# The last output piece of an attention kernel: 128 columns copied by VectorE in place of 256 copied by ScalarE

## Chip, core, metric

The kernel runs on one NeuronCore of a Trainium2 chip. The metric is device microseconds (us) of that core, median of several executions. Time before the change: 343.14 us (three runs, 342.83 to 343.26).

## The reference

Two independent attention blocks A and B with the same shapes; the outputs are concatenated along the last axis.

```python
# B, Sq, D = 16, 32, 1024;  Hq, Hkv, Sk, Dh = 32, 4, 512, 128;  all bf16
q = (x @ wq).reshape(B, Sq, Hq, Dh).transpose(0, 2, 1, 3)
k = repeat(k_cache, 8, axis=1); v = repeat(v_cache, 8, axis=1)
p = softmax(einsum("bhqd,bhkd->bhqk", q, k) * Dh ** -0.5)
o = einsum("bhqk,bhkd->bhqd", p, v)
out = o.transpose(0, 2, 1, 3).reshape(B, Sq, Hq * Dh) @ wo        # (16, 32, 1024)
# result: concatenate([out_A, out_B], -1)
```

## The kernel before

A generator `stream()` feeds projection matmuls into TensorE between the attention matmuls. Its last units are the output projection of B, token tile by token tile. A unit multiplies all 32 heads' `oT` blocks (each loaded as weights) with up to 512 columns of `wo`, sums in PSUM, copies the sum to SBUF as bf16 and writes it out.

```python
outp = enter(tc.tile_pool(name="outp", bufs=2))
...
def f_units(pr, tt, n0, width, eng):
    ps = psum.tile([P, NW], FP32, name="f_ps", tag="proj")        # P = 128, NW = 512
    nh, off = divmod(n0, NW)
    for h in range(HQ):                                           # HQ = 32
        ...
        nc.tensor.matmul(ps[:, 0:width], lhsT=oT[pr, tt][:, h, :],
                         rhs=wo_tiles[pr, nh, h // REP][:, h % REP, off:off + width],
                         start=(h == 0), stop=(h == HQ - 1))
        if h == HQ - 1:
            o_sb = outp.tile([P, NW], BF16, name="o_sb")
            nc.scalar.copy(out=o_sb[:, 0:width], in_=ps[:, 0:width])
            ...
            eng.dma_start(out=out_flat[tt * P:(tt + 1) * P, c0:c0 + width], in_=o_sb[:, 0:width])
        yield
...
    yield from f_units(1, TT - 1, 0, NW, nc.sync)                 # the last three units
    yield from f_units(1, TT - 1, NW, QW, nc.sync)                # QW = 256
    yield from f_units(1, TT - 1, NW + QW, QW, nc.scalar)
```

After that every engine compares one number (`ok`, a check of the softmax sums) and branches: in the normal case over a long general path to the end of the program. So each engine that has run out of work takes one branch.

```python
tc.mark_branch_hint_location("general", "LikelyTaken",
    [nc.scalar.engine, nc.vector.engine, nc.tensor.engine, nc.gpsimd.engine])
ok = nc.values_load(ok_i[0:1, 0:1], ...)
run(units, 1 << 20)                       # the rest of stream(), the pieces above among it
...
with tc.If(ok < total, preferred_fallthrough_block=True, label="general"):     # line 678
    general_path(tc, problems, out_flat)
```

## Time and profile before

The page of the profiled execution: the span, busy time per engine, the chain that ended last by engine, and two groups (line, engine, operation, tiles, shapes, count, then busy us and mean ns of one, then idle time before them).

```profile
span 341.2 us, 5454 instructions
...
PE 335.2 (98%) x2082; PEld 213.6 (63%) x2121; DVE 265.5 (78%) x336; ACT 185.9 (54%) x209; POOL 46.7 (14%) x206
...
PE 98%; issue 1%; ACT 0%; ACTq 0%
...
L320 PE MATMUL f_ps<-wo_sb,oT 128*128 128x512 bf16 (+1 forms) x525 | 128.2, 366 | 0.6
...
L329 ACT CAST o_sb<-f_ps 128x512 bf16<-128x512 f32 (+1 forms) x17 | 9.5, 559 | 23.6 <-PE f_ps L320 23.6
```

The kernel is bound by TensorE (PE). The change can only win in what follows its last matmul. The timeline of the tail (start and duration in us, engine, line, operation):

```profile
336.34 1.80 PE L320 MATMUL f_ps<-wo_sb,oT 128*128 128x256 bf16 x15
...
338.22 0.37 ACT L329 CAST o_sb<-f_ps 128x256 bf16<-128x256 f32 x1 [3.12 <-PE f_ps L320]
338.62 0.37 ACTq L331 DMA_DIRECT2D out_dram<-o_sb  x1
```

The last output matmul ends at 338.14; this moment is called T below. Copy, issue of the write, then nothing in the timeline until the span ends at 341.22: T + 3.08. What fills the rest is seen in the DMA view, here for the window T - 1.2 to T + 2.8 us (40 slices of 0.1 us: busy tenths of the 16 DMA engines; then queues with packets and MB; then the write with its size and the us from issue to landing).

```profile
DMA  0050000000000000000000000188200300000000
...
q10 hardware_dynamic: 144, 0.07, 5.5%
q8 instruction: 1, 0.02, 1.5%
q14 instruction: 1, 0.01, 0.8%
...
out_dram<-o_sb ACTq DMA_DIRECT2D x1, 64.0 KB, 1.6
```

The 144 packets on q10 are the last write: 128 rows of 512 bytes and 16 semaphore updates, inferred to be one per DMA engine (16 of each; the shares are of 8 rows, 128 / 16, and one update). They pass in slices 26 to 29. A landing is the moment at which such an update arrives; I count a write as complete with the last of its 16, because SyncE's closing wait ended 0.016 us behind that one here (landings at T + 1.947 to 2.102).

### The profile page before, as it was taken

To read this page: it belongs to the slowest core of one execution; us is meant where nothing else is said; L and a number is where in the kernel's file an instruction comes from. 1 tells how busy PE (TensorE), PEld (TensorE's weight loads), DVE (VectorE), ACT (ScalarE), POOL (GpSimd) and SP (SyncE) were. 2 spreads that over 40 slices of the span, in tenths; PEclk is the share of its full clock that TensorE was granted. 3 is DMA by queue.
4 is the path that set the end of the run, shared out by engine and by line. 5 is a ranking of instruction groups with operands and counts; after the bars stand their busy time and mean duration, and the time that the engine had idled before them with its cause. 6 is when DMAs were issued, how large, how long until landed. Compare 5 with 4: busy or idle time off the path is not lost.

```text
span 341.2 us, 5454 instructions
## 1 busy us (share of the span) xinstructions
PE 335.2 (98%) x2082; PEld 213.6 (63%) x2121; DVE 265.5 (78%) x336; ACT 185.9 (54%) x209; POOL 46.7 (14%) x206
## 2 busy tenths in 40 slices
PE   8999999999999999999999999999999999999996
PEld 6455666666666666666666666666666666666555
DVE  1046988888988898888888988879888888889540
ACT  3058666666667667666645545555555555555110
POOL 0001110011111111110012221222122101111100
PEclk9999999999999999999999999999999999999999
DMA  7999999999996987899999955998449997430001
GB/s 211 287 190 273 285 249 202 233 242 268 291 248 154 232 242 219 210 314 299 308 306 258 250 125 144 334 268 242 118 103 296 356 187 176 104 97 16 18 18 33
DMA packets 128094, 71.70 MB, mean 210 GB/s; under 512 B 75840, under 2 KB 127296, under 8 KB 128064
## 3 DMA queue, kind: packets, MB, share of 16 engines
q1 hardware_dynamic: 127264, 70.07, 84.1%
q0 software_dynamic: 384, 1.05, 0.9%
q8 instruction: 17, 0.28, 0.3%
q10 hardware_dynamic: 416, 0.20, 0.2%
q14 instruction: 13, 0.11, 0.1%
HBM read 50.86 MB, written 2.10 MB: 155 GB/s over the span
## 4 chain that ended last, share of the span: by engine, by line
PE 98%; issue 1%; ACT 0%; ACTq 0%
PE f_ps L320 32%; PE q_ps L301 28%; PE ob L425 17%; PE s_ps L357 16%; PE q_ps L534 4%; PE q_ps L516 1%; PE xT_ps L524 0%; ACT o_sb L329 0%; ACTq L329 0%
## 5 line engine op out<-in xcount | busy, mean ns | idle before, releaser
L365 ACT ACTIVATE p_sb<-s_ps,shift 128x1024 bf16<-128x1024 f32 x128 | 142.7, 1115 | 97.5 <-PE s_ps L357 88.1
L376 DVE TRANSPOSE_TENSOR_REDUCE parts<-p_sb 128x32 f32<-128x1024 bf16 x128 | 158.7, 1240 | 21.0 <-ACT p_sb L365 19.3
L320 PE MATMUL f_ps<-wo_sb,oT 128*128 128x512 bf16 (+1 forms) x525 | 128.2, 366 | 0.6
L301 PE MATMUL q_ps<-xT,wq_sb 128*128 128x512 bf16 x430 | 113.2, 379 | 0.5
L425 PE MATMUL ob<-p_sb,v_sb 128*128 128x256 bf16 x512 | 76.8, 273 | 0.8
L357 PE MATMUL s_ps<-qT,kT 128*128 128x256 bf16 x512 | 76.8, 273 | 0.0
L320 PEld LDWEIGHTS <-oT 128*128 128x128 bf16 x544 | 53.2, 98 | 35.3
L357 PEld LDWEIGHTS <-kT 128*128 128x128 bf16 x512 | 56.9, 113 | 28.3
L301 PEld LDWEIGHTS <-wq_sb 128*128 128x128 bf16 x448 | 43.8, 98 | 32.2
L425 PEld LDWEIGHTS <-v_sb 128*128 128x128 bf16 x512 | 50.1, 98 | 20.0
L447 DVE TENSOR_TENSOR oT<-r,ob 128x512 bf16<-128x512 f32 x64 | 43.9, 686 | 19.9 <-PE ob L425 19.4
L411 DVE STREAM_TRANSPOSE r<-rall 128x512 f32<-128x512 f32 x64 | 44.2, 691 | 1.1
L309 ACT CAST qT<-q_ps 128x512 bf16<-128x512 f32 x56 | 32.7, 583 | 16.5 <-PE q_ps L301 16.5
L394 POOL COPY half<-cs 64x32 f32<-64x32 f32 x32 | 6.5, 204 | 231.8 <-DVE cs L384 231.8
L329 ACT CAST o_sb<-f_ps 128x512 bf16<-128x512 f32 (+1 forms) x17 | 9.5, 559 | 23.6 <-PE f_ps L320 23.6
L534 PE MATMUL q_ps<-xT,w_sb 128*128 128x512 bf16 (+1 forms) x65 | 14.4, 379 | 0.1
L384 DVE TENSOR_REDUCE cs<-parts 128x32 f32<-128x128 f32 x32 | 12.1, 377 | 1.1
L406 DVE RECIPROCAL rall<-sums 128x32 f32<-128x32 f32 x32 | 10.2, 319 | 3.3 <-POOL sums L403 3.3
L534 PEld LDWEIGHTS <-w_sb 128*128 128x128 bf16 x67 | 6.8, 102 | 7.0 <-DMA w_sb<-in_A_wq_dram 0.2
L560 DVE CAST qT<-q_ps 128x512 bf16<-128x512 f32 x4 | 2.5, 684 | 10.2 <-PE q_ps L534 10.2
L331 POOL DMA_DIRECT2D out_dram<-o_sb x8 | 4.6, 574 | 29.3 <-ACT o_sb L329 29.3
L395 POOL TENSOR_TENSOR half<-half,cs 64x32 f32<-64x32 f32 x32 | 7.8, 243 | 2.6
(25 smaller groups left out, 44.7 us busy)
## 6 DMA issues: line engine op xcount, KB each, us to landing
v_sb<-in_A_v_cache_dram SPq DMA_DIRECT2D x16, 512.0 KB, 5.7
wq_sb<-in_B_wq_dram SPq DMA_DIRECT2D x8, 1024.0 KB, 5.7
wo_sb<-in_A_wo_dram SPq DMA_DIRECT2D x8, 1024.0 KB, 7.4
v_sb<-in_B_v_cache_dram SPq DMA_DIRECT2D x16, 512.0 KB, 4.7
wo_sb<-in_B_wo_dram SPq DMA_DIRECT2D x8, 1024.0 KB, 8.1
wq_sb<-in_A_wq_dram SPq DMA_DIRECT2D x5, 1024.0 KB, 5.8
wq_sb<-in_A_wq_dram SPq DMA_DIRECT2D x2, 512.0 KB, 6.7
kT<-in_A_k_cache_dram SPq DMA_TRANSPOSE x64, 4.4
```

The lines of the kernel that those rows point to most:

```text
L301: nc.tensor.matmul(ps[:], lhsT=w[:, dc, (h % 4) * DH:(h % 4 + 1) * DH], rhs=xT[pr][:, dc, :], start=(dc == 0), stop=(dc == DC - 1),)
L309: nc.scalar.copy(out=qT[pr, g][:, :, hl, :], in_=ps[:].rearrange("p (b s) -> p b s", s=SQ),)
L320: nc.tensor.matmul(ps[:, 0:width], lhsT=oT[pr, tt][:, h, :], rhs=wo_tiles[pr, nh, h // REP][:, h % REP, off:off + width], start=(h == 0), ...
L357: nc.tensor.matmul(s_ps[:, c, :], lhsT=kT[:, i % GRP, c, :], rhs=qT[pr, g][:, b, :, :].rearrange("p h s -> p (h s)"), start=True, stop=True,)
L365: nc.scalar.activation(out=p_sb[:], in_=s_ps[:], func=ACTF.Exp, bias=shift[:], scale=SCALE)
L376: nc.vector.tensor_reduce(out=parts[k][:, q, :, :].rearrange("p c h -> p (c h)"), in_=st[i]["p"][:].rearrange("p c (h s) -> p (c h) s", s=SQ),
L384: nc.vector.tensor_reduce(out=cs[:], in_=parts.pop(k)[:].rearrange("p q c h -> p q h c"), axis=AX.X, op=ALU.add,)
L406: nc.vector.reciprocal(out=rall[:, k, :], in_=quad.pop(k)[:])
L411: nc.vector.transpose(out=r[:].rearrange("p n s -> p (n s)"), in_=rall[:, k, o * 2 * REP:(o + 1) * 2 * REP] .unsqueeze(2).to_broadcast([P, ...
L425: nc.tensor.matmul(ob[j][:, q, :], lhsT=v_sb[:, i % GRP, c, :], rhs=st[i]["p"][:, c, :], start=(c == 0), stop=(c == KC - 1),)
L447: nc.vector.tensor_tensor(out=out, in0=rcp.pop(j)[:].rearrange("p (q h) s -> p q h s", h=REP), in1=ob.pop(j)[:].rearrange("p q (h s) -> p ...
L534: nc.tensor.matmul(first_q[h][:, ts], lhsT=w0[dc // HC][:, dc % HC, h * DH:(h + 1) * DH], rhs=xT[0][:, dc, ts], start=(dc == 0 and t0 == 0 ...
```

## The change

The last piece becomes 128 columns and is copied by VectorE; the piece ahead takes 384. Intent: half the width makes the copy shorter, and the copy is exposed.

```diff
-            def f_units(pr, tt, n0, width, eng):
+            def f_units(pr, tt, n0, width, eng, copy=nc.scalar.copy):
...
-                        nc.scalar.copy(out=o_sb[:, 0:width], in_=ps[:, 0:width])
+                        copy(out=o_sb[:, 0:width], in_=ps[:, 0:width])
...
-                yield from f_units(1, TT - 1, NW, QW, nc.sync)
-                yield from f_units(1, TT - 1, NW + QW, QW, nc.scalar)
+                yield from f_units(1, TT - 1, NW, NW - P, nc.sync)
+                yield from f_units(1, TT - 1, 2 * NW - P, P, nc.scalar, nc.vector.tensor_copy)
```

## The prediction

> **What bounds it now.** The chain of waits is 98% PE (page, part 4); PE is busy 335.2 of 341.2 us at clock 1.00. The change touches only the tail. Timeline there: the 512-wide piece's last matmul leads into two 256-wide pieces of 32 matmuls, which start every 109 ns without a gap (331.10 to 337.98 us); the last matmul's modelled end is 338.14. Then, exposed: 0.08 us until ACT starts the copy (338.22; elsewhere ACT and DVE follow PE by 0.037), 0.373 us copy (128x256), 0.03 us to the DMA issue on ACT's queue (338.62), 0.37 us issue, 0.5 us until the first packet (339.50), 0.35 us of packets (144 on that queue, about 27 ns each over 16 engines), 0.4 us until SP's wait is released (340.26), and 0.96 us of closing barriers. So about 3.1 us follow PE, and only the copy and the transfer in it can change.
>
> **What changes.**
> - PE: 32 matmuls of 384 and 32 of 128 columns for 64 of 256. Starts are 215.7 ns apart at 512 columns and 109.2 at 256, so a line gives 162.5 at 384 and 56 at 128. The warm transposes at 6.8 us, 128 columns with a fresh weight load each, do start every 56 ns, so a weight load (98 ns long, overlapped) need not slow the stream. 32 x (162.5 + 56) = 6.99 us against 6.99: no change. [...]
> - Tail copy: ACT 128x256, 373 ns, becomes DVE 128x128. DVE's fp32 PSUM copy of 512 columns took 684 ns, its bf16 ones 291 (256) and 424 (512), a fixed part near 155 ns; [...]estimate 155 + 128 x 1.04 = about 285 ns. ACT itself would need about 265 (373 and 587 extrapolated). So the width saves, not the engine: -0.09 us.
> - Waits: the DVE copy waits on eight DMA semaphores, PE and ACT. Those are old writers and readers of its buffer, done long before; DVE is idle from 330.3 us, so they are off the chain. PE to DVE should be the same 0.08 us, DVE to ACT's queue 0.03.
> - DMA: still 128 rows, 256 instead of 512 bytes. Issue and packet count stay, so hardly shorter. [...]no 256-byte output write is in this trace. I allow 0 to +0.15 us.
> - The 384-wide piece ends about 1.7 us later: matmuls to 336.4, ACT copy about 0.48, issue until about 337.3, landed near 338.6. Ahead of the last landing (340.26), so off the chain.
>
> **Sum.** 0 (PE) - 0.09 (copy) + 0.04 (transfer) = -0.05 us. Predicted 343.1 us, 8 in 10 between 342.7 and 343.6. Faster by over 2%: 0.5%; within 2%: 99%; slower: 0.5%.
>
> **Right if** the timeline shows 128-column matmuls starting every 56 ns, PE's end within 0.05 us of before, the DVE copy at 0.27 to 0.30 us, starting 0.08 us after PE's end, and first packet to SP's release staying near 0.75 us.
>
> **Wrong if** PE spaces the 128-column pairs by 70 ns or more (PE end +0.5 us or later); if DVE works through its many waits after PE's end rather than before (+0.3 us); if 256-byte writes complete noticeably later; or if DVE's late branch ends after SP's final wait. The run-to-run spread, 0.4 us, is larger than the expected gain, so the sign may not be readable.

The +0.04 for the transfer, out of the allowance of 0 to +0.15, was the author's estimate, and no trace showed it; so was the +0.3 for late waits. The 1.04 ns per column of the copy agree with the trace of before: (684 - 155) / 512 = 1.03.

## The result

The changed kernel took 344.26 us (six runs, 344.03 to 344.95) against 343.2 us (six runs, 342.83 to 343.48): 1.0034 times as long, 95% interval 1.0021 to 1.0047. Ratios here are the mean time of one kernel's fast runs over that of the other's fast runs of the same rounds, so not quite the ratio of the medians quoted. It is within 2%, but slower by 1.06 us in the medians where 0.1 us less was predicted, and outside the stated range.

The page after, which is of the slowest of the six runs (344.95 us), first the lines that answer to those of before:

```profile
span 343.0 us, 5497 instructions
...
PE 337.9 (99%) x2121; PEld 212.6 (62%) x2121; DVE 265.8 (77%) x337; ACT 185.7 (54%) x208; POOL 46.7 (14%) x206
...
DVE 0%
DVE o_sb L329 0%
...
L320 PE MATMUL f_ps<-wo_sb,oT 128*128 128x512 bf16 (+2 forms) x544 | 132.3, 366 | 0.0
...
L329 ACT CAST o_sb<-f_ps 128x512 bf16<-128x512 f32 (+1 forms) x16 | 9.2, 577 | 22.2 <-PE f_ps L320 22.2
```

The chain breaks off at VectorE's copy, because the view puts that copy's wait down to TensorE's sequencer. It is the ordinary wait for the last matmul. The larger PE busy time is a count of records: the trace of before lacks 39 matmul records (2082 of 2121). The timeline of the tail:

```profile
337.26 1.78 PE L320 MATMUL f_ps<-wo_sb,oT 128*128 128x128 bf16 x29
337.34 0.48 ACT L329 CAST o_sb<-f_ps 128x384 bf16<-128x384 f32 x1 [4.61 <-PE f_ps L320]
...
337.84 0.34 SPq L331 DMA_DIRECT2D out_dram<-o_sb  x1
339.14 0.29 DVE L329 CAST o_sb<-f_ps 128x128 bf16<-128x128 f32 x1 [9.37 <-PEq L678]
339.46 0.37 ACTq L331 DMA_DIRECT2D out_dram<-o_sb  x1
```

T is 339.04 here, and the span ends at 343.05: T + 4.01 in place of T + 3.08. The DMA view for the window T - 1.2 to T + 2.8:

```profile
DMA  0000000039968000000000000660103010000000
...
q10 hardware_dynamic: 144, 0.03, 3.9%
q8 instruction: 1, 0.02, 1.8%
q14 instruction: 2, 0.02, 1.3%
...
out_dram<-o_sb SPq DMA_DIRECT2D x1, 96.0 KB, 1.6
out_dram<-o_sb ACTq DMA_DIRECT2D x1, 32.0 KB, 2.6
```

Half the bytes take 2.6 us from issue to landing instead of 1.6. And there are two instruction packets on q14 in this window instead of one. Term by term, in us, from the records of the two traces and of a second profile of the changed kernel (the run after_again below, there the fastest of five, 343.95 us). The prediction counts its last two terms from the release of SyncE's wait, which follows the last landing by 0.02 us; hence 0.98 here for its 0.96:

```
                                   before   predicted   after   after_again
T to start of the copy              0.080     0.08      0.094      0.092
copy                                0.373     0.285     0.292      0.292
end of copy to issue                0.030     0.03      0.031      0.033
issue                               0.368     0.37      0.368      0.367
end of issue to first packet        0.506     0.5       0.508      0.505
first packet to last landing        0.745   0.75-0.9    1.735      1.424
last landing to end of span         0.978     0.98      0.978      0.979
sum: T to end of span               3.080     3.0-3.15   4.006      3.692
```

One line is wrong, by 0.7 to 1.0 us; all others hold within 0.015 us.

The spans of the two profiles differ by 1.83 us, of which 0.93 is this tail. The other 0.90 arose before the first output matmul (at 169.75 us before, 170.65 after; from there to T both took 168.39 us). In the trace's clock records the full TensorE clock was granted at 5.09 us in the one and 6.63 in the other. Over the 13 profiles (of 14) with such a record (T 337.93 to 339.04) T is earliest where the grant came earliest (3.72 us) and latest where it came latest (6.63). As this part lies ahead of all changed code, I take it for spread from run to run and not for part of the change; no run tests that. It blurs all times below by 1 us or so; the tail after T, from the profiles, is the sharper measure.

What the packets of the last write show: of its 128 rows 120 pass between T + 1.29 and T + 1.55 us, as they should. The remaining 8, with one of the 16 semaphore updates, by that count one DMA engine's share, begin only at T + 1.986. One instruction packet on q14, of 8192 bytes, lies at T + 1.682 to T + 1.989 in the same trace. In the trace of before no instruction packet falls between T and the end of the write's packets. The records also show the branch of each engine (line 678): VectorE's ended at T - 8.54 us before and at T + 0.20 after, because its copy now comes ahead of the branch; TensorE's at T - 1.71 and T - 0.75. Some 1.1 us after a branch of VectorE, and 0.72 to 0.81 us after TensorE's, an instruction packet follows: q14, 8192 bytes, and q8, 16384 bytes. (Which engine a fetch belongs to is inferred from this fixed distance, which all experiments repeated; VectorE's in this one profile came after 1.48 us.) SyncE takes the same branch, but no instruction packet follows its branch in any of the 14 profiles; it is the one engine that is missing from the branch hint's list in the source above.

### The profile page after: what moved, and what is told of

It reads as the page before. It is cut to its first block, busy times and chain, and to the rows that moved or that the text cites. A ratio compares the mean times of both kernels' runs of the same rounds, so it can differ in the third digit from the quotient of the medians.

```text
span 343.0 us, 5497 instructions
## 1 busy us (share of the span) xinstructions
PE 337.9 (99%) x2121; PEld 212.6 (62%) x2121; DVE 265.8 (77%) x337; ACT 185.7 (54%) x208; POOL 46.7 (14%) x206
## 5 line engine op out<-in xcount | busy, mean ns | idle before, releaser
L320 PE MATMUL f_ps<-wo_sb,oT 128*128 128x512 bf16 (+2 forms) x544 | 132.3, 366 | 0.0
L301 PE MATMUL q_ps<-xT,wq_sb 128*128 128x512 bf16 x448 | 116.9, 379 | 0.0
L320 PEld LDWEIGHTS <-oT 128*128 128x128 bf16 x544 | 52.0, 98 | 36.7
L534 PE MATMUL q_ps<-xT,w_sb 128*128 128x512 bf16 (+1 forms) x67 | 15.4, 390 | 0.2 <-DMA w_sb<-in_A_wq_dram 0.2
```

The costliest lines, as they stand in the source:

```text
L301: nc.tensor.matmul(ps[:], lhsT=w[:, dc, (h % 4) * DH:(h % 4 + 1) * DH], rhs=xT[pr][:, dc, :], start=(dc == 0), stop=(dc == DC - 1),)
L320: nc.tensor.matmul(ps[:, 0:width], lhsT=oT[pr, tt][:, h, :], rhs=wo_tiles[pr, nh, h // REP][:, h % REP, off:off + width], start=(h == 0), ...
L534: nc.tensor.matmul(first_q[h][:, ts], lhsT=w0[dc // HC][:, dc % HC, h * DH:(h + 1) * DH], rhs=xT[0][:, dc, ts], start=(dc == 0 and t0 == 0 ...
```

## The experiments

Three theories. F: VectorE's late branch brings an instruction fetch that holds one DMA engine just when the last write arrives. S: 256-byte writes complete later. P: TensorE's own fetch does it, which is later because its last 32 pairs pass faster (56 ns apart instead of 109). The first two experiments undo one half of the change each. The diffs below are cuts: against the changed kernel, but those of dve256, late_touch, early_touch and pe_late against the kernel before.

**act128: the width alone**

```diff
-  yield from f_units(1, TT - 1, 2 * NW - P, P, nc.scalar, nc.vector.tensor_copy)
+  yield from f_units(1, TT - 1, 2 * NW - P, P, nc.scalar)
```

> The changed kernel with ScalarE copying the last 128 columns again: the width part of the change alone. Theory F (fetch): in the changed kernel VectorE takes its final branch only after the last copy, and the instruction fetch that follows a branch by about 1.07 us holds one of the 16 DMA engines just when the last output packets reach it; with ScalarE copying, VectorE branches 8 us earlier, so F expects 343.1 us (343.2 before, minus 0.1 for the shorter copy), 16 landings close together. Rival S (size): 256-byte writes finish about 1 us later than 512-byte ones; expects 344.2. Rival P: TensorE's own fetch, 1.9 us later because the last 32 weight and matmul pairs pass faster, is in the way; expects 344.2 as well.

Measured: 343.55 us, ratio to before 0.9999 (0.9985 to 1.0013). No 8 packets stay behind. The last landing is at T + 2.395, the other 15 by T + 1.864; the span ends at T + 3.37. So S falls: the write has 256-byte rows and its time is that of before, and 15 of its 16 landings are earlier than any of before (1.947 to 2.102). F's expectation was missed in one point: it had all 16 landings close together, and one is 0.53 us behind the others. P can explain that part at most: TensorE's fetch lasted until T + 1.367 here, past the first packets (T + 1.252). No rows are held, but a few are slow, up to 0.153 us where most take 0.018, and the last update of the write passes only at T + 1.722.

**dve256: the engine alone**

```diff
-  yield from f_units(1, TT - 1, NW + QW, QW, nc.scalar)
+  yield from f_units(1, TT - 1, NW + QW, QW, nc.scalar, nc.vector.tensor_copy)   # 256 and 256, as before
```

> Two last pieces of 256 columns as before, the last one copied by VectorE: the engine part alone. F: VectorE's fetch falls about 1.2 us after the end of the matmuls, the packets of the last write about 1.4 to 1.75 us after it (copy about 0.42 us); the fetch was held up until 1.7 us in the changed kernel, so F expects a delay of the same kind, 0.2 to 1.1 us slower than before, 343.4 to 344.3. S and P expect 343.25 (only a copy longer by 0.05 us).

Measured: 344.03 us, ratio 1.0014 (1.0001 to 1.0027). VectorE's fetch is at T + 1.304 to 1.892, one engine's 8 packets begin at T + 1.889, the last landing is at T + 2.906 and the span ends at T + 3.885, 0.80 later than before; the copy itself (0.424 us) is 0.05 longer. VectorE's part alone, with 512-byte rows and TensorE's fetch out of the way (over by T - 0.03), does nearly all of the damage.

**own_tile: one wait instead of ten on VectorE's copy**

```diff
+  o_last = const.tile([P, P], BF16, name="o_last")
-  o_sb = outp.tile([P, NW], BF16, name="o_sb")
+  o_sb = own if own is not None else outp.tile([P, NW], BF16, name="o_sb")    # own=o_last for the last piece
```

> The changed kernel with the last 128 columns copied by VectorE into a buffer of its own, so that this copy waits for one semaphore (TensorE) and VectorE's sequencer can pass it and branch about 8 us earlier, as TensorE's does. F expects 343.05 us (copy 0.08 shorter, one wait fewer), the fetch near 331.5 us in the trace, the 16 landings together. S and P expect 344.2.

Measured: 343.81 us, ratio 1.0009 (0.9997 to 1.0021). The premise failed: TensorE's branch ends ahead of its last matmul (T - 0.75 in after), but VectorE did not branch ahead of its waiting copy, its branch ended at T + 0.135, so the collision stayed (fetch T + 1.241 to 1.735, the 8 packets from T + 1.731, last landing T + 2.613, end T + 3.59). As a test of the theories it tells nothing new. It did show that the copy starts at T + 0.037 when it waits for one semaphore, instead of T + 0.094.

**hold: useless work on VectorE after its copy**

```diff
+  junk = const.tile([P, 20], FP32, name="junk")
   run(units, 1 << 20)
+  for n in range(20):
+      nc.vector.memset(junk[:, n:n + 1], 0.0)
```

> The changed kernel with 20 one-column memsets on VectorE after its copy, work that nobody waits for: VectorE's branch comes 0.5 to 1.5 us later, so its fetch should come after the packets of the last write (over 1.7 us after the end of the matmuls). F expects 343.1 to 343.5 us, faster than the changed kernel although more is done. S and P expect 344.2 or more.

Measured: 343.73 us, ratio 1.0004 (0.9991 to 1.0017). VectorE's branch ended at T + 0.765 and its fetch began at T + 1.885, behind the write's packets; no 8 packets stayed behind, the last landing was at T + 2.351, the end at T + 3.33 instead of 4.01 and 3.69 in the changed kernel. More work, a shorter tail, and in time the interval lies below the changed kernel's (1.0021 to 1.0047), though the median missed the 343.1 to 343.5 that F expected. F holds, S falls again. The last landing is still 0.45 behind the 15th; TensorE's fetch lasted until T + 1.323 here.

The next three add a suspect to the kernel before and leave its output path as it is.

**late_touch and early_touch: only the time of VectorE's branch**

```diff
+  if touch:                                # ahead of the piece's matmuls
+      nc.scalar.copy(out=mark[0:1], in_=shift[0:1])
   ...
+  if touch:                                # after the piece's write is issued
+      t_ps = psum.tile([P, 1], FP32, name="t_ps", tag="ob")
+      nc.tensor.matmul(t_ps[:], lhsT=warm, rhs=warm[:, 0:1], start=True, stop=True)
+      nc.vector.tensor_copy(out=mark[0:1], in_=t_ps[0:1])
   # touch=True for the last piece (late_touch) or for the piece ahead of it (early_touch)
```

> The kernel before, its output path untouched (two pieces of 256, ScalarE copies), with one thing added: after the last matmul of the last piece TensorE does a one-column matmul, VectorE copies one element of it to a scratch tile, and only then branches. Nobody waits for either. Theory F: VectorE's fetch lands near 1.2 to 1.5 us after the last output matmul, on top of the packets of the last write (1.36 to 1.7); last landing at 2.5 to 3.0 us after it instead of 2.10, kernel 0.4 to 0.9 us slower. If the copy by VectorE itself or the width were the cause: 2.10 as before, 343.3 us.

> Control: the same matmul and VectorE copy, after the piece ahead of the last. VectorE branches about 3.4 us before the end of the matmuls; its fetch falls near 2.3 us before it, in nobody's way. F: last landing 2.10 us after the last matmul as before, kernel within 0.15 us of before.

Measured: late_touch 344.0 us, ratio 1.0027 (1.0012 to 1.0042); early_touch 343.64 us, ratio 1.0014 (0.9999 to 1.0028). These intervals overlap, and early_touch's median is 0.31 us above that of before, where 0.15 at most was expected; so the times do not separate the two. The profiles do. Timeline of late_touch, T = 338.43:

```profile
338.26 0.17 PE L340 MATMUL t_ps<-const-bfloat16-1.0 128*128 128x1 bf16 x1
338.51 0.37 ACT L332 CAST o_sb<-f_ps 128x256 bf16<-128x256 f32 x1 [3.04 <-issue]
338.57 0.15 DVE L343 COPY mark<-t_ps 1x1 f32<-1x1 f32 x1 [9.41 <-PEq L687]
338.91 0.37 ACTq L334 DMA_DIRECT2D out_dram<-o_sb  x1
```

And its DMA view for T - 1.2 to T + 2.8:

```profile
DMA  0005000000000000000000000588200300000000
...
q10 hardware_dynamic: 144, 0.07, 5.6%
q14 instruction: 2, 0.02, 1.8%
...
out_dram<-o_sb ACTq DMA_DIRECT2D x1, 64.0 KB, 2.3
```

The copy and the issue stand at T + 0.08 and T + 0.48 as before, but a one-element copy that nobody waits for makes VectorE branch at T + 0.25: a second packet on q14 appears and the same 64 KB write takes 2.3 us instead of 1.6. The fetch lies at T + 1.372 to 1.979, one engine's 8 packets begin at T + 1.975, the last landing is at T + 2.759, the span ends at T + 3.737. In early_touch VectorE branches at T - 3.27; its DMA view has the lines of before again:

```profile
DMA  0080000000000000000000000188200400000000
...
q14 instruction: 1, 0.01, 1.0%
...
out_dram<-o_sb ACTq DMA_DIRECT2D x1, 64.0 KB, 1.6
```

Last landing T + 2.105 (2.102 before), end T + 3.084 (3.080 before). Same added instructions, 0.65 us apart in the tail.

**pe_late: only the time of TensorE's branch**

```diff
   run(units, 1 << 20)
+  idle_ps = psum.tile([P, P], FP32, name="idle_ps", tag="ob")
+  for _ in range(20):
+      nc.tensor.matmul(idle_ps[:], lhsT=warm, rhs=warm, start=True, stop=True)
```

> The kernel before with 20 warm 128-column matmuls added on TensorE after the last piece, read by nobody: TensorE reaches its branch about 1.1 to 1.8 us later. Theory P': TensorE's 16 KB instruction fetch in the tail follows its branch by 0.75 us; it would move from 0.96 us before the end of the output's matmuls to 1.0 to 1.4 us after it, into the packets of the last write, and the last landing would move from 2.10 to 2.5 us or later. Rival: this fetch is one of a regular series (one about every 20 us)[...]; then it stays near 0.96 us before that end and the last landing stays at 2.10.

Measured: 344.93 us, ratio 1.005 (1.0036 to 1.0064). DMA view, T - 1.2 to T + 2.8:

```profile
DMA  0000000000000000000000700188200300000000
...
q10 hardware_dynamic: 142, 0.07, 6.1%
q8 instruction: 1, 0.02, 2.0%
...
out_dram<-o_sb ACTq DMA_DIRECT2D x1, 64.0 KB, 2.9
```

TensorE's branch moved to T + 0.375 and its fetch with it, from T - 0.962 to T + 1.094 until 2.348. One engine's 8 packets begin at T + 2.334; two of the write's 144 packets even fall out of the window. The last landing is at T + 3.383 and the end at T + 4.36. So a fetch of TensorE does the same harm when it overlaps the write, and more: it took 1.254 us against 0.3 to 0.7 of VectorE's, and the landing came 0.36 us later than in any other run. The rival, that this fetch is one of a regular series (17 packets on q8 in the 341.2 us of before, a mean of 20 us), falls for this run.

**hold_both: useless work on both engines**

```diff
   run(units, 1 << 20)                      # of the changed kernel
+  idle_ps = psum.tile([P, P], FP32, name="idle_ps", tag="ob")
+  for _ in range(38):
+      nc.tensor.matmul(idle_ps[:], lhsT=warm, rhs=warm, start=True, stop=True)
+  for n in range(20):
+      nc.vector.memset(junk[:, n:n + 1], 0.0)
```

> The changed kernel with useless work on both engines after their last real instruction: 20 memsets on VectorE, 38 matmuls on TensorE, so that both branch later and both fetches should come after the packets of the last write. If both fetches follow the branches and both hurt: last landing near 2.0 us after the output's last matmul (1.83 to 1.9 for the first 14 of 16 seen in act128 and hold), closing barriers about 1 us later, kernel 343.1 or less. If TensorE's fetch is of the regular series, the last landing stays near 2.35 to 2.4 as in hold.

A miss: 344.63 us, ratio 1.004 (1.0026 to 1.0054). With the 38 matmuls came a further fetch on q8 that has no branch ahead of it (T + 0.628 to 1.934), in the write's way: 8 packets from T + 1.919, last landing T + 2.962. TensorE's branch came only at T + 3.32, 1.1 us after its last idle matmul, and a second fetch on q8 followed at T + 4.08; the end was at T + 4.46. That end follows from TensorE's late branch and not from the last landing: SyncE's closing wait for TensorE lasted until T + 3.46. Padding TensorE is no remedy.

**after_again, act128_again, sp_issue**

after_again and act128_again repeat the changed kernel and act128 for a second profile. sp_issue takes ScalarE's branch, and so its fetch, away from the end of the changed kernel:

```diff
-  yield from f_units(1, TT - 1, 2 * NW - P, P, nc.scalar, nc.vector.tensor_copy)
+  yield from f_units(1, TT - 1, 2 * NW - P, P, nc.sync, nc.vector.tensor_copy)
```

> The changed kernel once more, beside the others of this job. The same tail is expected: TensorE's fetch starting 0.0 us and VectorE's 1.3 to 1.7 us after the last output matmul, 14 of the 16 landings by 1.9, the last at 2.7 to 3.1 us, against 2.10 before; the time 0.2 to 0.5% above before.

> Width part alone once more. VectorE's fetch is far away; TensorE's starts at 0.0 and ScalarE's at 1.86 us after the last output matmul. Expected: 15 landings by 1.9, the last at 2.2 to 2.5 us; the time within 0.15% of before.

> The changed kernel with the last write issued by SyncE, so that ScalarE branches about 2 us earlier and its fetch falls near 0 instead of 1.9 us after the last output matmul. VectorE and TensorE as in the changed kernel. If ScalarE's fetch takes part in the late landing: last landing at 2.2 to 2.6 us instead of 3.03. If only VectorE's and TensorE's do: 2.7 to 3.1 still.

Measured: after_again 344.61 us, ratio 1.0034 (1.0021 to 1.0047), fetch of VectorE T + 1.308 to 1.887, 8 packets from T + 1.883, last landing T + 2.713. sp_issue 344.4 us, ratio 1.0028 (1.0015 to 1.0041), ScalarE's fetch at T - 0.608 and yet 8 packets from T + 1.956, the end of VectorE's fetch (1.960), last landing T + 2.953: ScalarE's fetch takes no needed part. act128_again 343.62 us, ratio 1.001 (0.9996 to 1.0024): TensorE's fetch took 0.958 us this time and was over at T + 0.985, ahead of the write's first packet; last landing T + 2.013, end T + 2.991. The last landing was expected at 2.2 to 2.5, so this is a miss. The end is 0.09 us better than before, just what the prediction had hoped for from the width, but in one profile; the times do not show it. The three profiles with 128 columns and VectorE's fetch clear of the write (act128, hold, act128_again) suggest that it is then down to the length of TensorE's fetch (0.958 to 1.366 us in the seven profiles that start it near T) whether the write is disturbed.

**act192_own: a version made after these findings**

```diff
+  o_last = const.tile([P, 192], BF16, name="o_last")
-  yield from f_units(1, TT - 1, NW, NW - P, nc.sync)
-  yield from f_units(1, TT - 1, 2 * NW - P, P, nc.scalar, nc.vector.tensor_copy)
+  yield from f_units(1, TT - 1, NW, NW - 192, nc.sync)
+  yield from f_units(1, TT - 1, 2 * NW - 192, 192, nc.scalar, nc.scalar.copy, o_last)
```

> Last piece 192 wide, the one ahead 320, ScalarE copies the last into a buffer of its own (one wait instead of three). VectorE branches 8 us ahead; TensorE's last pairs start every 82.5 ns, so its branch ends about 1.2 us and its fetch starts about 0.45 us before the last output matmul ends, over by 0.9. The copy should start 0.04 us after it (0.08 before) and take 0.32 us (0.373 before). With no fetch in the way the last landing comes at about 2.0 us (2.10 before), the end at 2.98 (3.08 before): 0.1 us better than both kernels, which the times, 0.4% apart from run to run, can hardly show.

Measured: 343.14 us, ratio to before 0.9996 (0.9984 to 1.0008). Timeline, T = 337.93, and the write's line of the DMA view:

```profile
337.96 0.32 ACT L330 CAST o_last<-f_ps 128x192 bf16<-128x192 f32 x1 [2.17 <-PE f_ps L321]
338.31 0.37 ACTq L332 DMA_DIRECT2D out_dram<-o_last  x1
```

```profile
q14 instruction: 1, 0.01, 0.9%
...
out_dram<-o_last ACTq DMA_DIRECT2D x1, 48.0 KB, 1.6
```

TensorE's fetch lies at T - 0.502 to T + 0.767, the landings at T + 1.804 to 1.949, the end at T + 2.927: 0.15 us less than before in one profile. The times can't confirm that; they do show it faster than the changed kernel (0.9996 against 1.0034, intervals apart).

All 14 profiles in one table, us after T, from the trace's records. "Held" is where the last group of 8 row packets and one semaphore update, one engine's share, begins, if it stays behind the others; -7.4 and -2.1 are the starts of fetches that were long over.

```
               VectorE's fetch   TensorE's fetch   held from   last landing   end of span
before         -7.4              -0.962 to -0.003     -           2.102          3.080
early_touch    -2.1              -0.980 to  0.414     -           2.105          3.084
act192_own     -7.4              -0.502 to  0.767     -           1.949          2.927
act128_again   -7.4               0.027 to  0.985     -           2.013          2.991
act128         -7.4               0.001 to  1.367     -           2.395          3.374
hold            1.885 to 2.387    0.037 to  1.323     -           2.351          3.329
own_tile        1.241 to 1.735    0.007 to  1.154   1.731         2.613          3.592
after_again     1.308 to 1.887    0.054 to  1.323   1.883         2.713          3.692
late_touch      1.372 to 1.979   -0.852 to  0.106   1.975         2.759          3.737
dve256          1.304 to 1.892   -0.985 to -0.026   1.889         2.906          3.885
sp_issue        1.306 to 1.960    0.012 to  1.247   1.956         2.953          3.932
after           1.682 to 1.989    0.012 to  1.147   1.986         3.028          4.006
hold_both       1.879 to 2.335    0.628 to  1.934   1.919         2.962          4.460
pe_late        -7.4               1.094 to  2.348   2.334         3.383          4.362
```

(ScalarE's fetch is left out; in hold and hold_both it lies at the same place as VectorE's, so the two may be swapped there.) In all eight profiles with a held share it begins within 0.02 us of the end of a fetch: of VectorE's in six, of TensorE's in hold_both and pe_late. In the six profiles without one, no fetch of VectorE or TensorE overlaps the write's packets by more than 0.12 us. That is why I call the cause shown. Why a fetch keeps the share waiting no trace shows. In all profiles but hold_both the span ended 0.978 or 0.979 us after the last landing; so one held share out of 16 holds up the end, here by 0.5 to 1.3 us (hold_both aside, where TensorE's late branch set the end).

The tails fit the times: in 12 of the 13 profiles other than before, the change of the tail against before lies in the 95% interval of the change in time (estimate: ratio less 1, times 343 us). The exception is after_again, 0.61 us of tail against 1.17 (0.72 to 1.61). The other profile of the changed kernel has 0.93 against the same 1.17. So 0.2 to 0.6 us of its slowdown is not located.

What stays open. The trace does not name the DMA engine of a packet; that the held share and the fetch are on the same one is inferred from their times. It does not show why a held share, once through, takes 0.5 to 0.9 us to land where the write before took about 0.4. TensorE's share in the changed kernel's delay is not fully separable: against act128_again, act128 lost 0.4 us in its one profile. Where TensorE's fetch starts near T and VectorE's follows it (own_tile, after_again, sp_issue, after), two landings are late, the 15th by 0.27 to 0.44 us behind the 14th; with VectorE's alone (late_touch, dve256) only the last is. So TensorE's fetch seems to delay a second share, not the one that lands last. And no run removed the fetches, or took an engine out of the branch hint to see whether its fetch goes away.

## Why the prediction was wrong

- The step that failed is the term "DMA: ... hardly shorter", with its allowance of "0 to +0.15 us" and the statement that "first packet to SP's release" stays "near 0.75 us". It measured 1.42 and 1.74 us up to the last landing. The prediction looked at the write alone (rows, bytes, packet length) and not at what else the same DMA engines would be doing at that moment.
- "Wrong if ... DVE's late branch ends after SP's final wait" saw that the branch moves, but asked only whether VectorE would be late itself. It was not: its branch ended at T + 0.20, 2.8 us ahead of that wait. The harm came through what follows a branch, the fetch.
- The sum "-0.09 (copy) + 0.04 (transfer) = -0.05" was therefore about -0.08 (copy) + 0.7 to 1.0 (transfer). act128_again, where no fetch interfered, did end 0.09 us earlier than before: the gain is there in that one profile, and the new collision eats it up to ten times over.
- "PE: no change" was right: the 128-column pairs start every 55 to 56 ns, the 384-column ones every 162 to 163, and from the first output matmul to T both kernels took 168.39 us.
- The copy (0.285 predicted, 0.292 measured), its start (0.08 and 0.094) and the hand-over to ScalarE's queue (0.03 and 0.031) were right. The many waits of the copy were indeed worked off ahead: of its five wait records in after, four were over by T - 4.5 us; the wait for TensorE and one more together cost 0.057 us against a copy with a single wait (own_tile).
- The doubt about 256-byte writes was not borne out: in act128_again all 16 landings came by T + 2.013, earlier than before.
- The range of 0.9 us was built on run-to-run spread and the known terms; it had no room for a new wait.

## What to carry to other kernels

At the end of a kernel look at every transfer on the DMA engines, not at your own write alone: in these runs each engine but SyncE brought an instruction fetch 0.7 to 1.5 us after its branch, and one fetch that meets the share of one DMA engine out of 16 held up the completion of the whole last write, by 0.5 to 1.3 us in eight of the 14 profiles. So give the last piece of work to an engine that is at its end anyway, let all others reach their branch early, and check the DMA view for packets of kind "instruction" in the write's window. If a 0.1 us saving shows up as a 1 us loss, compare the packet times of the last transfer before doubting the arithmetic of the compute engines.

## Also measured

- VectorE did not wait for the packet that followed its branch: its next instruction came 0.525 us after the branch, the packet 1.11 us (before) and 1.48 us (after). What those 0.525 us went into no run shows. The cost was one for the DMA engines: TensorE's packets were 16384 bytes on q8 and took 0.96 to 1.39 us; those after VectorE's and ScalarE's branches were 8192 bytes on q14 and took 0.3 to 0.7 us. Those that met the last write delayed its last landing by 0.5 to 1.3 us.
- 256-byte rows to the output showed no later completion: packets of 18 ns instead of 27 (by byte that is slower, 14 against 19 bytes per ns), and 0.61 us from the first packet to the 15th landing (act128) against 0.72 for 512-byte rows (before).
- Copies of 128 columns from PSUM: VectorE's took 292 ns (after), ScalarE's 267 (act128).
